# Reordering the first stage of an attention and MLP-mixer kernel

## The chip, the cores and the metric

The kernel runs on one NeuronCore of a Trainium2 chip, launched once. The metric is device time in microseconds of one execution. Five engines run side by side, each with its own instruction list: TensorE (PE) multiplies matrices, VectorE (DVE) and ScalarE (ACT) work on tiles in SBUF and PSUM, GpSimd (POOL) works on tiles in SBUF, and SyncE (SP) issues most of the DMA transfers. ACT and POOL issue transfers too. PE writes its results to PSUM, which has eight banks of 128 x 512 fp32.

## The reference

There are 8 batches, 8 heads, 576 positions and 64 elements per head. The first half is a linear attention with a norm, the second an MLP mixer:

```python
kv = np.einsum('bhsd,bhse->bhde', k, v)
out = np.einsum('bhsd,bhde->bhse', q, kv)
rms = np.sqrt(np.mean(out * out, axis=-1, keepdims=True) + 1e-06)
x = out / rms * g_norm                      # then (B, S, H*D) = 8 x 576 x 512
xt = x.transpose(0, 2, 1)
h = np.maximum(xt @ w_tok1, 0.0) @ w_tok2   # 576 -> 256 -> 576
u = x + h.transpose(0, 2, 1)
h2 = np.maximum(u @ w_ch1, 0.0) @ w_ch2     # 512 -> 1536 -> 512
return u + h2
```

The activations are fp32. The weights come in as 8-byte words and are turned to fp32 in the kernel.

## The kernel before

The batches are taken in pairs, four pairs in all. For a pair the kernel loads k, v and q, multiplies k and v to one 64 x 64 matrix per head (`kv`), evicts it (`evict`), multiplies q by it (`attend_tile`), squares and reduces the result to a root mean square, scales it to x, and then mixes tokens with w_tok1 and w_tok2. The last and longest part, the channel mixing with w_ch1 and w_ch2, follows for all batches. The change touches only the stage of the first pair, and what is loaded ahead of it.

A batch's k or v has 576 rows of 2 KB. The first 512 go to SBUF in one transfer, four rows to each of 128 partitions (8 KB pieces). The last 64 are the remainder, two transfers of 32 rows. `load(b)` issues them all: for batch 0 k on SP's queue and v on ACT's, for the others all on SP's. `load_q` fetches q's 512 positions (1 MB in 2 KB pieces), `load_q_rest` the other 64 (in 256 B pieces). Two batches have buffers at a time, so the loads of pair 1 wait for the products of pair 0.

A weight block is fetched as 8-byte words and decoded by five operations: two passes on ACT (`scale`), then `clamp`, `shift` and `add` on DVE. Before, w_tok1 has three blocks: rows 0 to 255, rows 256 to 511, and the remainder.

The order of the work in this stage is written out by hand. `start` is a list of step names that `play` takes one after the other. Each step puts its instructions at the end of its engines' lists, and each engine takes its list in order; an instruction waits by semaphores for what it reads. DMA transfers take eight semaphores in turn, so a transfer cannot be issued before the eighth one ahead of it has landed. The step names that matter, with side s (batch in the pair), tile c of x (two tiles of 128 positions for each c; c = 0, 1 are batch 0, c = 2, 3 batch 1, c = 4 the remainders) and half t:

- `kv`s h and `e`s h: the k and v products of one half of the heads, and their eviction.
- `a`c t: the product with q for one tile, into a PSUM bank of the pool "o", which has two.
- `g`c t: DVE multiplies the bank by g_norm into x (L453). `q`c t: ACT squares the bank (L457). `t`c t: DVE sums the squares (L474).
- `m`, `r`, `i`: mean on DVE (L479), square root on ACT (L484), inverse with one correction step on DVE (L488 to L493).
- `s`, `p` or `d` c t: x times the inverse, on ACT (eight instructions, L507), GpSimd (L515) or DVE (L511).
- `h`s t j: one product of w_tok1's block j with tile j of x, into a bank of the pool "h", which has four.
- `w`n k: step k of decoding block n (0 and 1 are w_tok1's two blocks, 2 its remainder, 3 and 4 w_tok2). `w`n 0 fetches.
- `l`, `lq`, `lr`: loads for the next pair. `gs` spreads g_norm over the partitions by a product with ones. `j`n: n products with an identity matrix whose result nobody reads.

Every PE product of fp32 operands is two records in the profile.

## Time and profile before

| what | us |
|---|---|
| three runs | 772.5, 770.87, 772.44 |
| median | 772.44 |
| profiled execution, its own time | 771.12 |
| its span, first to last instruction | 769.3 |
| PE busy in the span | 759.4 |
| DVE busy | 642.5 |
| ACT busy | 277.4 |
| GpSimd busy | 112.3 |

The first stage is the first 46 us or so. A line of the timeline gives the start, the time until the end of the last of the merged instructions, the engine, the line of the kernel, the operation, what it writes and reads, the count, and in brackets the idle time before it with what ended it. A line of the stretches gives the stretch, its length, busy time and instructions of PE, PE's weight loads, DVE, ACT and POOL, then the granted clock of PE, the busy share of the DMA engines and the rate in GB/s. Ends of matmuls are modelled, so a short wait of PE can be hidden in a row that looks busy; the spacing of starts shows it.

### The profile page before, as it was taken

Reading aid. Unit: us, or ns where it says so; the run is one execution under the profiler, and the core shown is the slowest. Engines: PE = TensorE matmul, PEld = TensorE weight load, DVE = VectorE, ACT = ScalarE, POOL = GpSimd, SP = SyncE. Lnnn points to the kernel's source line nnn. Section 1 sums busy time; section 2 is a strip of 40 time slices with the busy share of each in tenths; the row PEclk is TensorE's granted clock in tenths of the full one; section 3 lists DMA queues with packets and bytes.
Section 4 is the critical chain, followed back from the end, with each engine's and each line's share of the span. In section 5 each row is a group of like instructions: output and inputs, shape, how many; then the busy total and the mean of one; then the engine's idle time right before and its main releaser. Section 6 shows DMA issues by size and latency. Waiting matters only on the chain.

```text
span 769.3 us, 12678 instructions
## 1 busy us (share of the span) xinstructions
PE 759.4 (99%) x4676; PEld 612.3 (80%) x4676; DVE 642.5 (84%) x945; ACT 277.4 (36%) x556; POOL 112.3 (15%) x125
## 2 busy tenths in 40 slices
PE   7999999999999999999999999999999999999998
PEld 6665555445888888888888888888888888888887
DVE  3868897997767779899969889987998996798996
ACT  3555575764210233511244242123352223325221
POOL 1003020213410000002240001042000218000204
PEclk9999999999999999999999999999999999999999
DMA  9999998499699786589998577999659879955679
GB/s 339 366 366 370 373 372 301 151 318 342 251 286 339 271 282 191 164 270 207 216 236 251 158 224 216 255 188 267 202 148 290 172 220 208 207 145 157 151 200 119
DMA packets 137677, 188.26 MB, mean 245 GB/s; under 512 B 48658, under 2 KB 95250, under 8 KB 135570
## 3 DMA queue, kind: packets, MB, share of 16 engines
q1 hardware_dynamic: 101744, 167.54, 68.9%
q0 software_dynamic: 34816, 18.36, 16.1%
q10 hardware_dynamic: 1058, 1.57, 0.6%
q8 instruction: 37, 0.61, 0.3%
q14 instruction: 22, 0.18, 0.1%
HBM read 138.28 MB, written 49.15 MB: 244 GB/s over the span
## 4 chain that ended last, share of the span: by engine, by line
PE 97%; DMA 2%; SPq 0%; issue 0%; DVE 0%
PE ps_d L136 28%; PE ps_b L136 19%; PE ps_a L136 19%; PE ps_u L136 8%; PE ps_h L136 8%; PE ps_v L136 5%; PE ps_c L136 3%; DMA v_in<-in_v_dram 2%; PE ps_kv L136 2%; PE ps_o L136 2%; PE ps_w L136 2%; SPq L124 0%; PE ps_r L136 0%; DVE xs L127 0%
## 5 line engine op out<-in xcount | busy, mean ns | idle before, releaser
L136 PE MATMUL ps_d<-ui,w 128*128 128x256 f32 x504 | 118.6, 379 | 0.0
L136 PEld LDWEIGHTS ps_d<-ui,w 128*128 128x128 f32 x504 | 95.9, 190 | 12.9
L133 ACT COPY ps_d<-ps_a 128x768 f32<-128x768 f32 (+1 forms) x56 | 32.0, 572 | 200.2 <-PE ps_a L136 197.2
L127 DVE TENSOR_TENSOR v<-v,v 128x1536 f32<-128x1536 f32 (+2 forms) x70 | 103.2, 1482 | 0.3
L136 PE MATMUL ps_b<-sv,w 128*128 128x256 f32 x324 | 78.9, 380 | 0.0
L136 PE MATMUL ps_a<-v,w 128*128 128x256 f32 x324 | 78.8, 379 | 0.0
L1206 POOL DMA_DIRECT2D out_dram<-us x24 | 26.7, 1833 | 291.8 <-ACT p L133 286.2
L136 PEld LDWEIGHTS ps_b<-sv,w 128*128 128x128 f32 x324 | 61.3, 190 | 8.8 <-issue 0.6
L136 PEld LDWEIGHTS ps_a<-v,w 128*128 128x128 f32 x324 | 61.7, 190 | 8.2
L136 PE MATMUL ps_u<-h,w_tok 128*128 128x512 f32 (+1 forms) x160 | 64.7, 599 | 0.0
L136 PE MATMUL ps_d<-v,w 128*128 128x256 f32 x258 | 62.7, 379 | 0.0
L130 ACT ACTIVATE v<-v 128x768 f32<-128x768 f32 (+1 forms) x54 | 42.6, 822 | 55.1 <-DVE v L127 52.3
L136 PE MATMUL ps_h<-x,w_tok 128*128 128x512 f32 x128 | 57.8, 600 | 0.7 <-DVE w_tok L190 0.7
L1206 POOL DMA_DIRECT2D out_dram<-r x40 | 41.3, 1927 | 102.0 <-ACT p L133 80.3
L136 PE MATMUL ps_d<-sv,w 128*128 128x256 f32 x228 | 55.4, 379 | 0.0
L136 PEld LDWEIGHTS ps_d<-v,w 128*128 128x128 f32 x258 | 49.0, 190 | 6.5
L136 PEld LDWEIGHTS ps_u<-h,w_tok 128*128 128x128 f32 (+1 forms) x160 | 25.6, 179 | 31.1 <-issue 26.7
L136 PEld LDWEIGHTS ps_d<-sv,w 128*128 128x128 f32 x228 | 43.4, 190 | 5.8
L136 PE MATMUL ps_a<-uT,w 128*128 128x256 f32 x192 | 46.7, 379 | 0.0
L136 PEld LDWEIGHTS ps_h<-x,w_tok 128*128 128x128 f32 x128 | 23.4, 190 | 27.1 <-issue 24.1
L136 PE MATMUL ps_b<-ui,w 128*128 128x256 f32 x168 | 40.8, 379 | 0.0
L136 PEld LDWEIGHTS ps_a<-uT,w 128*128 128x128 f32 x192 | 36.5, 190 | 4.9
(169 smaller groups left out, 1288.0 us busy)
## 6 DMA issues: line engine op xcount, KB each, us to landing
w<-parts SPq DMA_DIRECT2D x168, 384.0 KB
w<-parts SPq DMA_DIRECT2D x56, 192.0 KB
uT<-blocks SPq DMA_DIRECT2D x36, 256.0 KB
k_in<-in_k_dram SPq DMA_DIRECT2D x8, 1024.0 KB
qT<-in_q_dram SPq DMA_DIRECT2D x8, 1024.0 KB
out_dram<-x POOLq DMA_DIRECT2D x16, 512.0 KB, 7.0
v_in<-in_v_dram SPq DMA_DIRECT2D x7, 1024.0 KB
raw<-in_moe_w_ch_dram SPq DMA_DIRECT2D x8, 768.0 KB
```

What stands on the lines that cost most here:

```text
L127: keep(engine.tensor_tensor(out=o, in0=a, in1=b, op=op))
L130: keep(nc.scalar.activation(o, a, AF.Relu))
L133: keep(nc.scalar.copy(o, a))
L136: keep(nc.tensor.matmul(*a, **kw))
L1206: keep(nc.gpsimd.dma_start(to, t()[ds(b * Q, Q), at].rearrange("p n l j -> p n (l j)"), accum_op=ALU.add))
```

## The change

- The loads of batch 0 all go on SP's queue, in this order: k's rows, v's rows, k's remainder, v's remainder. g_norm's row is fetched on POOL's queue instead of ACT's, ahead of everything else there.
- w_tok1's first block is split in two (rows 0 to 127 and 128 to 255). The first half is fetched after v's remainder and ahead of batch 0's q, the second after that q. The second block is fetched after batch 1's k and v instead of before them.
- `kv` is split by rows: `ka` multiplies the 512 rows, `kb` the remainder. Both halves of the heads do `ka` before `kb`.
- The second half of the first kv is evicted by ACT instead of DVE.
- For c = 0 and 1 the gain is taken apart: `y` copies the bank to x on ACT, `n` multiplies x by g_norm on GpSimd. DVE's `g` is gone there.
- The two tiles of c = 0 have statistics of their own (`m00`, `r00`, `i00` and `m01`, `r01`, `i01`) instead of common ones.
- `a10` and `a11` write to banks of the pool "h", so that the first four tiles have four banks.
- For c = 0 the second tile is scaled by GpSimd (`p01`) instead of ACT; for c = 1 the second tile by ACT (`s11`, placed after `q21`) instead of DVE. For c = 2 and 3 the square comes before the gain.
- The identity matrix is replaced by a full tile of ones, set by DVE. The unused products are 21, 5 and 4 instead of 12 and 8.

```diff
-    ident = inp.tile([P, P], F32, name="ident")
+    ones = inp.tile([P, P], F32, name="ones")
...
+    def load_rows(dst, t, b):
+        dma(dst[:, :J], t[b, :LO].rearrange("(p j) e -> p j e", j=J))
+
+    def load_rem(dst, t, b):
+        for n in range(0, HF, Q):
+            dma(dst[n:n + Q, J], t[b, LO + n:LO + n + Q].rearrange("(r e) d -> e r d", e=8))
...
-        queues = (nc.sync, nc.sync if b else nc.scalar)
-        for dst, t, e in zip((k_in[b % 2], v_in[b % 2]), (k, v), queues):
-            dma(dst[:, :J], t[b, :LO].rearrange("(p j) e -> p j e", j=J), e)
-            for n in range(0, HF, Q):
-                dma(dst[n:n + Q, J], t[b, LO + n:LO + n + Q].rearrange("(r e) d -> e r d", e=8), e)
+        pairs = ((k_in[b % 2], k), (v_in[b % 2], v))
+        if b:
+            for dst, t in pairs:
+                load_rows(dst, t, b)
+                load_rem(dst, t, b)
+        else:
+            for f in (load_rows, load_rem):
+                for dst, t in pairs:
+                    f(dst, t, b)
...
+    def get_tok1_half(j):
+        return block(DTOK, lambda raw: [(raw, words(moe_w_tok1)[ts(j, P)])], w_tok1[0][:, j])
...
-        def kv(side, half):
+        def kv(side, half, js=range(JJ)):
...
-                for j in range(JJ):
+                for j in js:
...
-            if whole and side == 0:
+            if whole and side == 0 and half == 0:
                 keep(nc.vector.tensor_copy(o, i))
             else:
                 copy(o, i)
...
-            o = ps["o"].tile([P, DM], F32, name="ps_o", tag="o")
+            n = "h" if c == 1 else "o"
+            o = ps[n].tile([P, DM], F32, name="ps_o", tag=n)
...
+        def take(c, h):
+            if (pair, c) not in X:
+                X[pair, c] = xps[pair % 2].tile([P, 2, DM], F32, name="x", tag="x2", bufs=4)
+            copy(X[pair, c][:, h].rearrange("p (h d) -> p h d", d=D), bank[c, h])
+
+        def gain_pool(c, h):
+            x = X[pair, c][:, h].rearrange("p (h d) -> p h d", d=D)
+            keep(nc.gpsimd.tensor_mul(x, x, g_sb.to_broadcast([P, H, D])))
...
+        alone = lambda c: whole and c == 0
...
+            if alone(c):
+                g = h
+                stat[g] = [stats.tile([P, H, 1], F32, name=name + str(h)) for name in ("ms", "root", "inv")]
+                keep(nc.vector.tensor_reduce(stat[g][0], sq[c, h], axis=AX.X, op=ALU.add))
+                return
...
+    first_rows = [get_tok1_half(j) for j in range(2)]
...
+    dma(g_row, bass.AP(tensor=g_norm.tensor, offset=g_norm.offset, ap=[[0, 1], list(g_norm.ap[0])]), nc.gpsimd)
     load(0)
+    first_rows[0][0]()
     load_q(0)
-    for block in tok1[:2]:
-        block[0]()
+    first_rows[1][0]()
     load(1)
+    tok1[1][0]()
     load_q(1)
...
     start = [
-        "j12 kv00 e00", "kv01 gs e01 l0", "a00 g00 q00", "a01 g01 q01 t00 t01 m0 w01",
-        "a10 w02 r0 i0 w03 d00 w04 q10 w30 w40 lq0", "a11 q11 s01 g10 g11 w11 j8",
-        "h000 h010 w12 w13 w14 t10 t11 m1 r1", "kv10 e10", "kv11 e11 i1 d10 d11 l1", "h001", "a20 q20", "h011",
-        "a21 q21 g20 g21 t20 t21 m2", "h002 h012 r2", "a30 g30 i2 d20 q30", "a31 q31 s21 g31 t30",
+        "j21 ka00 ka01 kb00 e00 kb01 e01 gs l0 w01 w02 w03 w04 j5",
+        "a00 q00 y00 n00 t00 m00 r00 i00 d00", "a01 q01 y01 n01 t01", "a10 q10 y10 n10 m01 r01 w51 i01 p01 w30 w40 lq0",
+        "a11 q11 y11 n11 w52 w53 w54 w11 t10 t11 m1 j4",
+        "h000 h010", "kv10 e10", "kv11 e11 r1 w12 w13 i1 d10 w14 l1", "h001", "a20 q20", "h011",
+        "a21 q21 s11 g20 g21 t20 t21 m2", "h002 h012 r2", "a30 q30 g30 i2 d20", "a31 q31 s21 g31 t30",
         "h003 h013 t31 m3",
         "a40 q40 r3 i3 d30 s31 g40 t40 m4 r4 w21 i4 d40 lr0 lr1"]
...
-            matmul(o[:, :P], lhsT=ident, rhs=ident, start=True, stop=True)
-
-    more |= {f"j{n}": do(keep_warm, n) for n in (8, 12)}
+            matmul(late["junk"][:, :P], lhsT=ones, rhs=ones, start=True, stop=True)
+
+    more |= {f"j{n}": do(keep_warm, n) for n in (4, 5, 21)}
```

In the new list block 0 is the first half of the old first block (`w0`), block 5 the second half (`w5`).

More of the change, by code (lines that the diff above doesn't have):

```diff
@@ L9 @@
 from concourse.dve_ops import ADD32_U16LIMBS
-from concourse.masks import make_identity
 F32 = mybir.dt.float32
@@ L97 @@
           for n, b in (("o", 2), ("kv", 2), ("h", 4))}
-    ident = inp.tile([P, P], F32, name="ident")
+    ones = inp.tile([P, P], F32, name="ones")
     g_sb = inp.tile([P, 1, D], F32, name="g_sb")
-    g_row, ones = (inp.tile([1, n], F32, name=name) for n, name in ((D, "g_row"), (P, "ones")))
+    g_row = inp.tile([1, D], F32, name="g_row")
     w_tok1 = [tokw.tile([P, 2, DTOK], F32, name=f"w_tok1{i}") for i in range(J // 2)]
@@ L164, in decode, with high, low, scale @@
         bits = dst.bitcast(U32)
-        def scale():
+        def high():
             keep(nc.scalar.activation(dst, raw()[..., 1].bitcast(F32), AF.Prelu,
                                       scale=2.0 ** -112, alpha=2.0 ** 32))
-            low = raw()[..., 0]
-            keep(nc.scalar.activation(low, low, AF.Copy, scale=2.0 ** -29))
+        def low():
+            t = raw()[..., 0]
+            keep(nc.scalar.activation(t, t, AF.Copy, scale=2.0 ** -29))
+        def scale():
+            high()
+            low()
         def scale_leaves():
@@ L190, in add @@
             keep(nc.vector._custom_dve(ADD32_U16LIMBS, out=o, in0=o, in1=flat().bitcast(U16)[..., 2 * leaves:][..., :2]))
-        return scale_leaves if leaves else scale, clamp, shift, add
+        return scale_leaves if leaves else scale, clamp, shift, add, high, low
     def words(w):
@@ L371, in attention @@
         whole = pair == 0
-        def kv(side, half):
+        def kv(side, half, js=range(JJ)):
             kk, vv = k_in[side], v_in[side]
-            if whole:
+            if js[0]:
+                o = kv_ps[side, half]
+            elif whole:
                 o = kv_ps[side, half] = zeroed[half]
@@ L378, in kv @@
                 o = kv_ps[side, half] = ps["kv"].tile([P, 2, P], F32, name="ps_kv", tag="kv")
+            split = len(js) < JJ
             for i in range(2):
-                for j in range(JJ):
+                for j in js:
                     for h in range(2):
@@ L384, in kv @@
                                rhs=vv[:, j, at],
-                               start=(j == 0), stop=(j == JJ - 1), skip_group_check=True)
+                               start=(j == 0 and not (split and i)), stop=(j == JJ - 1), skip_group_check=True)
         def evict(side, half):
@@ L495, in inv_of @@
         def inv_of(c, t):
+            if alone(c):
+                return stat[t][2].rearrange("p (k h) o -> p k h o", h=2)
             inv = stats_of(c)[2]
@@ L519, in attention @@
             for h in range(2):
-                steps |= {f"kv{s}{h}": do(kv, s, h), f"e{s}{h}": do(evict, s, h),
+                steps |= {f"ka{s}{h}": do(kv, s, h, range(J)), f"kb{s}{h}": do(kv, s, h, range(J, JJ)),
+                          f"kv{s}{h}": do(kv, s, h), f"e{s}{h}": do(evict, s, h),
                           f"l{s}": do(load, 2 * pair + 2 + s)}
@@ L532, in attention @@
                 steps |= {f"{n}{c}{t}": do(f, c, t) for n, f in zip("spd", (scale, scale_pool, scale_vector))}
+        if whole:
+            for h in range(2):
+                steps |= {f"m0{h}": do(mean, h), f"r0{h}": do(sqrt, h), f"i0{h}": do(invert, h)}
+                for c in range(2):
+                    steps |= {f"y{c}{h}": do(take, c, h), f"n{c}{h}": do(gain_pool, c, h)}
         for g in groups:
@@ L1250, in stream @@
         for n in range(len(blocks)):
-            clamp, shift, add = blocks[n][2:]
+            clamp, shift, add = blocks[n][2:5]
             if n + 1 < len(blocks):
@@ L1287 @@
     zeroed = [ps["kv"].tile([P, 2, P], F32, name="ps_kv", tag="kv") for _ in range(2)]
+    keep(nc.vector.memset(ones, 1.0))
     for t in zeroed:
@@ L1293 @@
     keep(nc.scalar.activation(root, root, AF.Sqrt))
-    make_identity(nc, ident)
-    keep(nc.gpsimd.memset(ones, 1.0))
-    dma(g_row, bass.AP(tensor=g_norm.tensor, offset=g_norm.offset, ap=[[0, 1], list(g_norm.ap[0])]), nc.scalar)
     def spread_g():
         o = ps["h"].tile([P, DM], F32, name="ps_g", tag="h")
-        matmul(o[:, :D], lhsT=ones, rhs=g_row, start=True, stop=True)
+        matmul(o[:, :D], lhsT=ones[:1], rhs=g_row, start=True, stop=True)
         copy(g_sb[:, 0], o[:, :D])
     start = [
[4 rows of a table removed]
[5 rows of a table added]
         "h003 h013 t31 m3",
@@ L1333 @@
     mixings.append(token_mixing(B // 2 - 1, range(2, 9), (0, 1)))
-    more = {f"w{n}{k}": f for n, b in enumerate(tok1 + tok2) for k, f in enumerate(b)}
+    more = {f"w{n}{k}": f for n, b in enumerate(first_rows[:1] + tok1[1:] + tok2 + first_rows[1:]) for k, f in enumerate(b)}
     more |= {f"f{n}": b[0] for n, b in enumerate(channel)}
@@ L1341, in keep_warm @@
     def keep_warm(n):
-        o = ps["h"].tile([P, DM], F32, name="ps_j", tag="h")
+        if n > 4:
+            late["junk"] = ps["h"].tile([P, DM], F32, name="ps_j", tag="h")
         for _ in range(n):
-            matmul(o[:, :P], lhsT=ident, rhs=ident, start=True, stop=True)
-    more |= {f"j{n}": do(keep_warm, n) for n in (8, 12)}
+            matmul(late["junk"][:, :P], lhsT=ones, rhs=ones, start=True, stop=True)
+    more |= {f"j{n}": do(keep_warm, n) for n in (4, 5, 21)}
     more["gs"] = spread_g
```

## The prediction

> **What bounds the kernel now.** I read the page first: TensorE (PE) is busy in 759.4 of 769.3 us, and the chain that ended last is 97% PE.

> ```profile
> span 769.3 us, 12678 instructions
> PE 759.4 (99%) x4676; PEld 612.3 (80%) x4676; DVE 642.5 (84%) x945; ACT 277.4 (36%) x556; POOL 112.3 (15%) x125
> PE   7999999999999999999999999999999999999998
> PE 97%; DMA 2%; SPq 0%; issue 0%; DVE 0%
> ```

> Only the first slice of PE is below 9, so whatever the first stage can give lies in the first 25 us. The change edits nothing behind that stage. If PE reaches some instruction x us earlier and never waits after it, the kernel ends x us earlier. The question is which instruction that is. PE's rows in the timeline, with the idle time in brackets:

> ```profile
> 8.81 0.69 PE L136 MATMUL ps_kv<-v_in,k_in 128*64 128x64 f32 x16 [0.85 <-DMA v_in<-in_v_dram]
> 12.19 2.05 PE L136 MATMUL ps_o<-kvp,qT 128*128 128x128 f32 x16
> 16.72 1.95 PE L136 MATMUL ps_j<-ident 128*128 128x128 f32 x16
> 19.35 1.99 PE L136 MATMUL ps_h<-x,w_tok 128*128 128x512 f32 x4 [0.68 <-DVE w_tok L190]
> 21.67 2.55 PE L136 MATMUL ps_kv<-v_in,k_in 128*64 128x64 f32 x80 [0.34 <-DMA v_in<-in_v_dram]
> 24.16 1.13 PE L136 MATMUL ps_h<-x,w_tok 128*128 128x512 f32 x2
> 25.24 1.13 PE L136 MATMUL ps_o<-kvp,qT 128*128 128x128 f32 x8
> 26.20 1.02 PE L136 MATMUL ps_h<-x,w_tok 128*128 128x512 f32 x2
> 27.07 1.05 PE L136 MATMUL ps_o<-kvp,qT 128*128 128x128 f32 x8
> ```

> The reader is to see the pair at 24.16 and 25.24: one product of two records, then `a20`, 1.08 us later. The same pair at 26.20 and 27.07 is 0.87 us apart. So `a20` waited about 0.2 us, which the model of matmul ends hides. `a20` is the first reader of q1 (batch 1's q). In the trace the semaphore of q1 has its last increment at 25.11, `a20`'s weight load starts at 25.21. Behind it PE's rows are spaced as their counts demand.

> Then the loads, by stretches (the last columns are granted clock, DMA share, GB/s):

> ```profile
> 3.00:7.00 4.00, 3.66 (x17) 3.66 (x18) 0.00 (x0) 1.49 (x2) 0.43 (x2) 1.00 1.02 408
> 10.50:13.50 3.00, 3.00 (x62) 2.87 (x58) 0.89 (x3) 0.21 (x1) 0.00 (x0) 1.00 0.99 305
> 13.50:19.50 6.00, 4.73 (x40) 4.35 (x39) 5.66 (x14) 5.03 (x14) 0.00 (x0) 1.00 1.03 412
> 19.50:22.50 3.00, 2.66 (x32) 1.38 (x34) 2.85 (x6) 1.52 (x4) 0.00 (x0) 1.00 1.03 380
> 22.50:25.20 2.70, 2.70 (x61) 1.88 (x57) 2.25 (x8) 0.85 (x3) 0.00 (x0) 1.00 1.22 268
> ```

> The DMA engines are full from 3 us on until q1 has landed. That is the second bound: what lands when is a matter of the bytes put ahead of it.

> **The change part by part.**

> Issue. ACT's three v0 issues go to SP, and a fourth load is put ahead of q0. SP took 2.07 us for its first three, so q0 is issued at about 0.75 + 6 x 0.69 + 0.45 = 5.3 us, not 2.87. Nothing is lost by it: the k0 and v0 rows, 2.1 MB at 408 GB/s from 2.5 us, hold the engines until 7.7. ACT's saved 2.4 us are worth nothing; ACT waits 7.6 us there until 12.30. [...]

> First kv. Before, 2.25 MB of k0 and v0 shared the engines with q0's start and PE began at 8.81, then waited 0.32 for remainders. Rows first: 8.3 to 8.8; I take 8.5, as the 42 junk records also end about there (DVE sets `ones` at 0.9 us, so from 1.1: 27 at the half-rate spacing of 0.213 until 6.88, when the trace shows the full clock, and 15 at 0.111, makes 8.5). The 80 records need 2.55 us, so kv ends at 11.1 instead of 11.83.

> q0. It has 0.26 MB of w_tok1 ahead of it that it had not: 0.64 us at 408 GB/s, 0.86 at the 305 of the stretch where w_tok1 was read. It landed at 12.02 and will at 12.7 to 12.9. `a00` starts at 12.9 instead of 12.19: 0.7 us later, and the five junk products wait in front of it for nothing.

> First x. From `a00` 12.9: product 1.0, square 0.60 (14.5), copy to x 0.6 on ACT (15.1); reduce 0.68 and mean 0.17 on DVE beside it (15.4), root 0.21, the four small operations of `i0` 0.85 (16.5). GpSimd's gain from 15.1 takes 1.25 (row of `p`, 1246 ns; 1.03 to 1.55 seen): 16.4. `d00` 0.69: 17.2. `h000`, which waited for the w_tok decode until 19.35, now starts at 17.2 to 17.9: 1.5 to 2.1 us earlier. The four PSUM banks end the 0.59 us wait for `sq` before `a10`. The extra statistics (five small DVE operations, 1.0 us) lie on a DVE that gives four gains (2.8 us) to GpSimd.

> Second kv. k1 and v1 have 0.52 MB less ahead of them: at 380 GB/s they land 1.4 us earlier, and kv10 starts at 20.3 instead of 21.67. `h000`, `h010` end by 19.7, so PE idles about 0.6 us. kv10, kv11 end at 22.9, `h001` (needs GpSimd's `p01`: `n10` and `p01` at 1.25 behind `i01` give 21) at 23.8.

> `a20`. Up to here PE is 1.4 us ahead. But q1 has ahead of it exactly the bytes of before: k0, v0, k1, v1 4.72 MB, q0 1.05, the 512 rows of w_tok1 1.05, and its own 1.05; only their order differs. The stretch was full before, so q1 lands at 25.1 again and `a20` starts at 25.2. PE's 1.4 us are spent as idle time in front of it. There is a second limit just below: ACT's `w11` now stands in front of `e10`, `e11` and waits for the second half of w_tok1, which lands right before q1: 21.9 to 22.4, plus 1.33 for the two decode passes, plus two copies of 0.36 gives 24.1 to 24.6.

> Behind `a20`. PE's list is the same to the end. On ACT `s11` (2.02) moves between `q21` and `q30`. From the rows: `q21` ends 28.82, `s11` 30.9, `r2` 31.2 (it waits for `m2` at 30.93 anyway), `q30` 31.8, `g30` on DVE 32.5, `i2` 0.98, `d20` 0.69: 34.2. Before, `d20` ended at 33.11; `h100` reads it at 34.30. Bounds 0 to 0.3 us; I take 0.05. `w14` ends by 27.2, `h002` wants it at 27.96.

> Junk: ten more products, all in waits of PE: 0.

> Sum: a20 from 25.24 to 25.2, plus 0.05: no change. Span 769.3, the profiled execution 771.1 again; that execution is 1.3 us below the median of 772.44, so I say 772.3 for a median.

> **Rivals.**

> B, q1 a little earlier. Its 16 increments come at 22.0 to 22.9 (seven) and 23.7 to 25.11 (nine), with 24.64 and 25.11 behind the rest. If the stragglers vanish, ACT's limit decides: -0.6 to -1.1 us, 771.4. For it: the last two look accidental. Against: nothing in the change takes bytes off the late engines.

> C, the whole advance passes. If q1 landed by 23.6, kv10's 1.4 us, or `h000`'s up to 2.1, would reach the end: 770.7. For it: 305 GB/s at 10.5 to 13.5 shows 0.3 MB, 0.75 us, lost while w_tok1 is read, and another order may lose less. Against: ACT's limit at 24.1 must fall too.

> D, slower: PE's clock. PE idles some 0.6 us before kv10 and up to 1.4 us before `a20`. At the start PE ran at half rate from 3.34 to 6.88. If the idle time brings that back once for as long, 3.5 us of work at half rate cost 1.75 us: 774.1. It decides from the point where the granted clock drops; the 0.85 us at 7.96 did not drop it, and the longest gap here is 1.4 us. [...]

> E, slower: ACT's queue. If w_tok1's second half lands after 23.1 (at the 268 GB/s of the last stretch), `w11` holds `e10`, `e11` past 25.2: landing at 24 puts `a20` at 26.1, +0.9, and up to +1.6 at 24.7: 773.5. Against: 19.5 to 22.5 ran at 380.

> That the loads don't change order can't be: SP's list is in program order.

> **How the numbers follow.** A, q1 decides: 0.58. B 0.17, C 0.12, D 0.06, E 0.07. A measurement of this kernel tells about 0.2% (1.5 us) from no change; the three runs of before spread over 1.6 us. Faster: C, a quarter of B, and 0.03 of A by scatter: 0.19. Slower: D, two thirds of E, and 0.03 of A: 0.14. The range goes from C's 770.7 to D's 774.0. A's own is 771.8 to 773.0.

> **What would show it.** After: kv's first row at 8.3 to 8.8; `a00` at 12.5 to 13.2; `h000` at 17 to 18; kv10 near 20.3; an idle stretch of PE of about 1.4 us that ends with `a20` at 25.0 to 25.5, released by qT; GpSimd rows of about 1.25 us; `h100` 9.1 us after `a20`; granted clock 1.00 throughout. `a20` before 24 means that q1 was not bound by bytes, and I am wrong towards faster. `a20` after 26, or a clock below 1.00 between 19 and 30, means slower.

## The result, and the profile after

| what | before | after |
|---|---|---|
| median, us | 771.33 (9 runs) | 773.62 (9 runs) |
| profiled execution, its own time | 771.12 | 772.95 |
| its span | 769.30 | 770.88 |

The changed kernel is slower: the ratio is 1.0026, with an interval of 1.0016 to 1.0036 that excludes 1; the medians are 2.3 us apart. Nine runs put the kernel before at 771.33; the median of 772.44 shown above came from three, two of them high. The profiled execution of the changed kernel is the fastest of its nine, so its 1.83 us over the profiled execution of before is a lower figure. The span gives 1.58 of them, what lies around the span 0.25.

The page of the changed kernel:

```profile
span 770.9 us, 12741 instructions
...
PE 762.0 (99%) x4696; PEld 614.2 (80%) x4696; DVE 643.9 (84%) x948; ACT 280.4 (36%) x564; POOL 118.9 (15%) x128
...
PE   8999999999999999999999999999999999999997
...
PE 96%; DVE 2%; DMA 1%; SPq 1%; issue 0%; ACT 0%; DVEq 0%
```

As before, only the first and the last slice of PE are below 9. But DVE now holds 2% of the chain that ended last, and SP's queue 1%; before both had 0%. PE's rows in the timeline of the changed kernel:

```profile
8.21 2.55 PE L135 MATMUL ps_kv<-v_in,k_in 128*64 128x64 f32 x80
...
13.09 3.81 PE L135 MATMUL ps_o<-kvp,qT 128*128 128x128 f32 x32 [0.65 <-DMA qT<-in_q_dram]
...
18.74 1.98 PE L135 MATMUL ps_h<-x,w_tok 128*128 128x512 f32 x4 [0.95 <-DVE x L552]
20.66 2.55 PE L135 MATMUL ps_kv<-v_in,k_in 128*64 128x64 f32 x80
24.41 1.10 PE L135 MATMUL ps_h<-x,w_tok 128*128 128x512 f32 x2 [1.20 <-DVE w_tok L206]
25.34 1.05 PE L135 MATMUL ps_o<-kvp,qT 128*128 128x128 f32 x8
...
28.77 1.98 PE L135 MATMUL ps_h<-x,w_tok 128*128 128x512 f32 x4 [0.63 <-DVE w_tok L206]
...
34.19 1.09 PE L135 MATMUL ps_r<-kvp,qR 128*64 128x128 f32 x16
```

PE's two waits in the first kv (0.85 us ahead of it, 0.32 for a remainder) are gone, and kv10 comes at 20.66 instead of 21.67, straight behind `h010`. `h001` (24.41) and `h002` (28.77) now wait for DVE's last step of a w_tok1 block, L206. `a20` (25.34) starts 0.43 us behind the second record of `h001`, the spacing of rows without a wait; in the trace q1's last increment is at 24.88 already. So it is L206, by way of `h001`, that sets `a20` here, and not q1. The last row, the first product of the remainders (`ps_r`), is the mark that I use for the end of the stage: from its start to PE's last matmul it is 732.28 us in the kernel before (33.27 to 765.55) and in the changed one (34.19 to 766.47). So the stage lost 0.92 us, and the other 0.66 us of the span lie behind PE's last matmul: 3.75 us before, 4.41 after.

The stretches of the changed kernel, with the columns as before:

```profile
3.00:7.00 4.00, 4.00 (x26) 4.00 (x25) 0.00 (x0) 0.00 (x0) 0.92 (x2) 1.00 1.01 426
10.50:13.50 3.00, 2.35 (x26) 2.05 (x22) 1.44 (x4) 1.23 (x4) 0.00 (x0) 1.00 1.07 418
13.50:19.50 6.00, 5.05 (x41) 4.58 (x40) 4.07 (x9) 3.22 (x7) 2.71 (x2) 1.00 1.00 403
19.50:22.50 3.00, 3.00 (x65) 2.04 (x65) 2.59 (x7) 2.62 (x7) 2.39 (x3) 1.00 1.08 360
22.50:25.20 2.70, 1.50 (x28) 1.05 (x23) 2.58 (x4) 0.99 (x3) 1.48 (x2) 1.00 1.14 264
```

The DMA engines are full all the way, the granted clock is full, and PE's idle time of 1.2 us before `h001` is the 1.50 busy of 2.70 in the last line. In the same line DVE is busy for 2.58 us with four instructions. Its rows in the timeline, and GpSimd's:

```profile
15.61 1.17 DVE L518 TENSOR_SCALAR ms<-ms 128x8 f32<-128x8 f32 x1
...
20.36 0.72 DVE L528 SCALAR_TENSOR_TENSOR ms<-ms,inv 128x8 f32<-128x8 f32 x1
...
21.71 1.15 DVE L201 TENSOR_SCALAR w_tok<-w_tok 128x256 uint32<-128x256 uint32 x1
22.97 1.29 DVE L206 CUSTOM_DVE_ANT_1 w_tok<-w_tok,raw 128x512 uint16<-128x512 uint16 x1
24.18 1.26 DVE L513 TENSOR_REDUCE ms<-sq 128x8 f32<-128x512 f32 x2
...
28.03 0.69 DVE L206 CUSTOM_DVE_ANT_1 w_tok<-w_tok,raw 128x1024 uint16<-128x1024 uint16 x1
```

```profile
15.48 1.27 POOL L485 TENSOR_TENSOR x<-x,g_sb 128x512 f32<-128x512 f32 x1 [11.56 <-ACT x L132]
18.05 2.99 POOL L485 TENSOR_TENSOR x<-x,g_sb 128x512 f32<-128x512 f32 x2 [1.31 <-ACT x L132]
21.66 1.05 POOL L556 TENSOR_TENSOR x<-x,inv 128x512 f32<-128x512 f32 x1 [0.61 <-DVE inv L532]
22.66 1.32 POOL L485 TENSOR_TENSOR x<-x,g_sb 128x512 f32<-128x512 f32 x1
```

A mean over 128x8 numbers (L518) takes 1.17 us, and it ends at 16.78, when GpSimd's multiplication ends (16.75). L528 ends at 21.08 with GpSimd's pair (21.04), L201 at 22.86, L206 at 24.26, each within 0.3 us of the end of a GpSimd row. Where GpSimd does nothing the same four take 0.17, 0.17, 0.29 and 0.43 (rows further down, of the runs without multiplications on GpSimd). With a second L518 of 0.52 that is 3.6 us in which DVE was held. What had begun ahead of the multiplication was not held: L552 at 18.00 took its 0.69 us, and there the multiplication, which began 0.05 us later, took 1.76 us instead of 1.27. DVE has no idle stretch over 0.3 us from 14.9 until 28.7: it has become the bound of the stage.

### The profile page after: what moved, and what is told of

Same layout as the page of the kernel before. It is cut to its first block, busy times and chain, and to the rows that moved or that the text cites. A ratio compares the mean times of both kernels' runs of the same rounds, so it can differ in the third digit from the quotient of the medians.

```text
span 770.9 us, 12741 instructions
## 1 busy us (share of the span) xinstructions
PE 762.0 (99%) x4696; PEld 614.2 (80%) x4696; DVE 643.9 (84%) x948; ACT 280.4 (36%) x564; POOL 118.9 (15%) x128
## 4 chain that ended last, share of the span: by engine, by line
PE 96%; DVE 2%; DMA 1%; SPq 1%; issue 0%; ACT 0%; DVEq 0%
PE ps_d L135 28%; PE ps_b L135 19%; PE ps_a L135 19%; PE ps_u L135 8%; PE ps_h L135 8%; PE ps_v L135 5%; PE ps_c L135 3%; PE ps_o L135 2%; PE ps_w L135 2%; PE ps_kv L135 2%; DMA qT<-in_q_dram 1%; SPq L123 1%; PE ps_r L135 0%; DVE w_tok L206 0%; DVE ms L518 0%; DVE w_tok L201 0%
## 5 line engine op out<-in xcount | busy, mean ns | idle before, releaser
L135 PEld LDWEIGHTS ps_h<-x,w_tok 128*128 128x128 f32 x128 | 23.3, 190 | 29.5 <-issue 23.8
```

What stands on the lines that cost most here:

```text
L135: keep(nc.tensor.matmul(*a, **kw))
```

## The experiments

Two theories of the stage. P: DVE is held by GpSimd's multiplications, and that makes the two waits for L206. L: DVE's list is too long or in a worse order by itself (ten small operations in place of five, decodes behind them). On the end behind PE's last matmul, T: PE's longer list brings one more fetch of instructions among the last stores; G: g_norm's row on another queue.

**The changed kernel once more, without an edit**

> The changed kernel once more, unchanged, to see what of its profile repeats. Theory P (DVE operations are held while GpSimd multiplies): DVE rows that overlap a GpSimd multiplication are stretched again (mean 1.2 us instead of 0.17, decode steps 1.1 to 1.3 us instead of 0.29 and 0.43), the product h001 waits about 1.2 us and h002 about 0.6 us for the w_tok decode, and the last PE row ends 0.9 us later than before. Theory L (DVE's list is merely longer and in a worse order): the two waits repeat, the stretched rows need not. Both: about 1.0025 of the kernel before. The tail behind the last PE row, 3.75 us before and 4.41 after in one profile each: if it is 4.4 again it belongs to the change, if it is near 3.8 it is scatter.

773.30 us, ratio 1.0024 (1.0015 to 1.0033); `h001` waits 1.19, `h002` 0.62, `ps_r` at 34.54, 4.02 us behind PE's last matmul. The waits repeat to 0.01 us; `ps_r` moves by 0.35, as the first q landed later (`a00` at 13.45 instead of 13.09). q1's last increment is at 24.90 and `a20` at 25.69, again 0.43 us behind the second record of `h001`.

**No multiplication on GpSimd**

```diff
-        "a00 q00 y00 n00 t00 m00 r00 i00 d00", "a01 q01 y01 n01 t01", "a10 q10 y10 n10 m01 r01 w51 i01 p01 w30 w40 lq0",
-        "a11 q11 y11 n11 w52 w53 w54 w11 t10 t11 m1 j4",
+        "a00 q00 g00 t00 m00 r00 i00 d00", "a01 q01 g01 t01", "a10 q10 g10 m01 r01 w51 i01 d01 w30 w40 lq0",
+        "a11 q11 g11 w52 w53 w54 w11 t10 t11 m1 j4",
```

> The changed kernel with the gain of the first four tiles back on DVE (one multiplication from the bank instead of copy on ACT and multiplication on GpSimd) and tile c=0, t=1 scaled by DVE: GpSimd does nothing in the stage, DVE does 3.4 us more. Theory P: no DVE row is stretched, 3.6 us of holding vanish, h001 does not wait for the decode, a20 starts at q1's landing (25.0 to 25.4), h002 at most 0.3 us late, and the kernel is 0.6 to 1.0 us faster than the changed one, about level with the kernel before. Theory L: DVE has 3.4 us more to do, h001 and h002 are later still, 1 to 3 us slower than the changed kernel.

772.65 us, ratio 1.0017 (1.0008 to 1.0026). From DVE's and PE's rows:

```profile
23.09 0.29 DVE L201 TENSOR_SCALAR w_tok<-w_tok 128x256 uint32<-128x256 uint32 x1
23.42 0.43 DVE L206 CUSTOM_DVE_ANT_1 w_tok<-w_tok,raw 128x512 uint16<-128x512 uint16 x1
```

```profile
23.90 1.13 PE L135 MATMUL ps_h<-x,w_tok 128*128 128x512 f32 x2 [0.77 <-DVE w_tok L206]
25.18 1.13 PE L135 MATMUL ps_o<-kvp,qT 128*128 128x128 f32 x8
...
28.28 1.98 PE L135 MATMUL ps_h<-x,w_tok 128*128 128x512 f32 x4 [0.22 <-DVE w_tok L206]
```

DVE has five operations more, 3.4 us of work, and yet ends its L206 earlier than in the changed kernel: no row is stretched. `h002` waits 0.22 instead of 0.63, and `ps_r` comes at 33.70. P had `h001` without a wait; it waits 0.77 us, but q1 covers that (last increment 25.04, `a20` 25.18). The work that GpSimd took off DVE cost DVE more than it saved.

**Three GpSimd multiplications more, read by nobody**

```diff
+    def extra():
+        keep(nc.gpsimd.tensor_mul(idle, idle, g_sb.to_broadcast([P, 6, D])))
...
-        "a00 q00 y00 n00 t00 m00 r00 i00 d00", "a01 q01 y01 n01 t01", "a10 q10 y10 n10 m01 r01 w51 i01 p01 w30 w40 lq0",
-        "a11 q11 y11 n11 w52 w53 w54 w11 t10 t11 m1 j4",
+        "a00 q00 y00 n00 px t00 m00 r00 i00 d00", "a01 q01 y01 n01 t01", "a10 q10 y10 n10 m01 r01 w51 i01 p01 w30 w40 lq0",
+        "a11 q11 y11 n11 px px w52 w53 w54 w11 t10 t11 m1 j4",
...
+    more["px"] = extra
```

> The changed kernel with three more GpSimd multiplications (128 x 384, about 0.95 us each) on a scratch tile that nobody reads: one behind the first gain, two behind the fourth. No instruction waits for them but GpSimd's own next ones, which have idle time ahead of them. Theory P: the correction step of the first inverse is held until the first extra one ends (d00 up to 0.8 us later), and mean, clamp and shift between 25 and 27 us are held by the other two: h002 waits 1 to 2 us more, the kernel 1 to 2 us slower than the changed one. Theory L: no change within 0.3 us.

774.43 us, ratio 1.0035 (1.0021 to 1.0049); `ps_r` at 35.61. DVE's list is unchanged, but `d00`, 0.69 us in the changed kernel, is held too, and `h000` comes at 20.14. `h002` waits 1.19 us, 0.56 more than in the changed kernel, where P had 1 to 2 more:

```profile
18.50 1.59 DVE L552 TENSOR_TENSOR x<-x,inv 128x512 f32<-128x512 f32 x1
```

**Common statistics for the first two tiles, as before**

```diff
-        alone = lambda c: whole and c == 0
+        alone = lambda c: False
...
-        "a00 q00 y00 n00 t00 m00 r00 i00 d00", "a01 q01 y01 n01 t01", "a10 q10 y10 n10 m01 r01 w51 i01 p01 w30 w40 lq0",
+        "a00 q00 y00 n00 t00", "a01 q01 y01 n01 t01 m0 r0 i0 d00", "a10 q10 y10 n10 w51 p01 w30 w40 lq0",
```

> The changed kernel with common statistics for the two first tiles, as before (five small DVE operations and one ACT root less). GpSimd's multiplications stay. Theory L: DVE's list is 1 us shorter and free of one round trip over ACT, h001 and h002 wait at least 1 us less, and the kernel comes to the level of the one before. Theory P: h000 is 1 to 2 us later, as it needs both tiles' sums; the GpSimd multiplications still hold two to four DVE operations for 1.5 to 3 us in all, and h002 is still late by 0.3 us or more.

773.19 us, ratio 1.0023 (1.0014 to 1.0032). Here `h000` comes at 20.18 and kv10 at 22.09, 1.4 us later than in the changed kernel. And yet `h001` and `h002` wait for nothing, and `ps_r` is at 33.50, earlier than there. DVE was still held (L197 1.13, L201 1.25 and L552 1.29 us), but its list had five small operations less and its decodes stood further ahead. (Its time is still above that of before: 4.65 us lie behind PE's last matmul.) So holding alone does not make the loss; it needs a list without room for it.

**The gains left out.** GpSimd's five multiplications are left out, so the first tiles of x lack the gain and `x01` its scale. All other lists are those of the changed kernel.

```diff
-        "a00 q00 y00 n00 t00 m00 r00 i00 d00", "a01 q01 y01 n01 t01", "a10 q10 y10 n10 m01 r01 w51 i01 p01 w30 w40 lq0",
-        "a11 q11 y11 n11 w52 w53 w54 w11 t10 t11 m1 j4",
+        "a00 q00 y00 t00 m00 r00 i00 d00", "a01 q01 y01 t01", "a10 q10 y10 m01 r01 w51 i01 w30 w40 lq0",
+        "a11 q11 y11 w52 w53 w54 w11 t10 t11 m1 j4",
```

> The changed kernel with GpSimd's five multiplications left out (the four gains and the scaling p01, so the first tiles of x are not multiplied); DVE's list, ACT's and PE's are those of the changed kernel. It prices the holding alone. Theory P: no DVE row between 14 and 24 us is longer than the same row alone (L518 0.17, L528 0.17, L201 0.29, L206 0.43 or 0.7 for the wide one), DVE's list is some 3 us shorter, h001 and h002 wait for no decode of w_tok, a20 at 25.0 to 25.4 (q1's bytes), ps_r at 33.2 to 33.6. Rival L (DVE's list is too long for the stage by itself): h001 or h002 still waits 0.4 us or more for w_tok and ps_r is at 33.9 or later.

772.32 us, ratio 1.0011 (1.0002 to 1.0019).

```profile
22.60 1.12 PE L135 MATMUL ps_h<-x,w_tok 128*128 128x512 f32 x2
25.38 1.13 PE L135 MATMUL ps_o<-kvp,qT 128*128 128x128 f32 x8 [1.65 <-DMA qT<-in_q_dram]
...
28.10 1.88 PE L135 MATMUL ps_h<-x,w_tok 128*128 128x512 f32 x4
...
33.41 1.09 PE L135 MATMUL ps_r<-kvp,qR 128*64 128x128 f32 x16
```

```profile
16.08 0.17 DVE L518 TENSOR_SCALAR ms<-ms 128x8 f32<-128x8 f32 x1
...
16.76 0.17 DVE L528 SCALAR_TENSOR_TENSOR ms<-ms,inv 128x8 f32<-128x8 f32 x1
...
20.20 0.29 DVE L201 TENSOR_SCALAR w_tok<-w_tok 128x256 uint32<-128x256 uint32 x1
20.61 0.42 DVE L206 CUSTOM_DVE_ANT_1 w_tok<-w_tok,raw 128x512 uint16<-128x512 uint16 x1
```

This is the prediction's own picture: `h001` directly behind kv11, then 1.65 us of idle time until q1 has landed, `a20` at 25.38, no wait for DVE. The stage ends 0.14 us behind that of before; what is left of the loss lies at the end, 4.77 us behind PE's last matmul. P holds and L alone falls: the list has room where it is not held. L206 ends at 21.03 here and at 24.26 in the changed kernel, 3.2 us apart, while kv11 ends at 22.6: there were 1.6 us to spare.

**Twenty unused products, as before the change**

```diff
-        "j21 ka00 ka01 kb00 e00 kb01 e01 gs l0 w01 w02 w03 w04 j5",
+        "j16 ka00 ka01 kb00 e00 kb01 e01 gs l0 w01 w02 w03 w04",
...
```

> The changed kernel with twenty junk products (sixteen and four) in place of thirty, as many as the kernel before has. Theory T (the end is later because PE's list is longer: a 38th packet of 16384 bytes on queue 8 lands at 764 us, among the last stores): that packet is gone, 37 are left with the last near 748, and the stretch from PE's last matmul to the end of the span is 3.7 to 3.9 us instead of 4.0 to 5.1; PE's last matmul at 766.4 to 766.9 as in the changed kernel, or later where the clock rises later for the missing junk; the time 0.3 to 1.2 us below the changed kernel's. Theory G (the end is later for another reason, such as g_row's fetch that left ACT's queue): the stretch stays at 4.0 to 5.1 us, whatever the packets do.

773.45 us, ratio 1.0027 (1.0016 to 1.0037): as slow as the changed kernel. The stretch behind PE's last matmul is 4.13 us. That is in G's range and not in T's, although the packet that T named is gone. The page's rows of the two instruction queues, before, after, and here:

```profile
q8 instruction: 37, 0.61, 0.3%
q14 instruction: 22, 0.18, 0.1%
```

```profile
q8 instruction: 38, 0.62, 0.3%
...
q14 instruction: 23, 0.19, 0.1%
```

```profile
q8 instruction: 37, 0.61, 0.3%
...
q14 instruction: 23, 0.19, 0.1%
```

That packet (16384 bytes on queue 8, 0.9 us of one DMA engine, at 764 us in the changed kernel) is no longer there, and the stores land as in the kernel before. The rest lies on SP, whose list is 855 entries long, not 850 (v0's three loads, one more for the split block, one wait). In all fifteen profiles the trace has a step of 0.36 to 0.38 us in front of SP's 848th entry. In the kernel before that is between the closing drains, where a step takes 0.16 us here. In the lists of 855 it falls among the closing waits, which are otherwise 0.06 to 0.09 us apart, and the drains follow with steps of their own. The last step is 0.46 us here and 0.23 in the kernel before; what it waits for is not shown. The 23rd packet on queue 14 (8192 bytes) is not one more: the page counts what starts inside the span, and the last packet starts at 770.60 here, 0.40 us ahead of the end, and at 769.55 in the kernel before, 0.25 us behind it. So T is half right: a second term, the length of SP's list, is added.

**g_norm's row back on ACT's queue**

```diff
-    dma(g_row, bass.AP(tensor=g_norm.tensor, offset=g_norm.offset, ap=[[0, 1], list(g_norm.ap[0])]), nc.gpsimd)
+    dma(g_row, bass.AP(tensor=g_norm.tensor, offset=g_norm.offset, ap=[[0, 1], list(g_norm.ap[0])]), nc.scalar)
```

> The changed kernel with g_row's fetch back on ACT's queue. Theory G: the stretch from PE's last matmul to the end of the span is back at 3.7 to 3.9 us, and the time 0.3 to 1.2 us below the changed kernel's. Theory T: the packet at 764 us is still there, the stretch is 4.0 to 5.1 us and the time level with the changed kernel's within 0.5 us.

773.46 us, ratio 1.0027 (1.0017 to 1.0036); the packet at 764 us is there and the stretch is 4.46 us. G falls.

**The kernel before with one part of the change: w_tok1's second block behind batch 1's k and v**

```diff
-    for block in tok1[:2]:
-        block[0]()
+    tok1[0][0]()
     load(1)
+    tok1[1][0]()
...
-        "a11 q11 s01 g10 g11 w11 j8", "h000 h010 w12 w13 w14 t10 t11 m1 r1", "kv10 e10", "kv11 e11 i1 d10 d11 l1",
+        "a11 q11 s01 g10 g11 j8", "h000 h010 t10 t11 m1 r1 i1 d10 d11", "kv10 e10", "kv11 e11 w11 w12 w13 w14 l1",
```

> The kernel before with one thing of the change: the second block of w_tok1 (half a megabyte) is fetched behind batch 1's k and v, and w11 to w14 moved behind e11; statistics, gains, banks and junk as before. Theory Q (the bytes ahead of batch 1's q decide when a20 starts): k1 and v1 land about 1.3 us earlier, kv10 starts at 20.9 to 21.3 as soon as h000 and h010 are done, PE then waits about 1 us, a20 at 25.0 to 25.5 as before; the time is level with the kernel before, within 0.3 us. Theory R (the order of loads gains by itself and only the work on DVE and GpSimd lost it): a20 before 24.6, the time 0.6 to 1.3 us below the kernel before.

771.26 us, ratio 1.0001 (0.9990 to 1.0013), level.

```profile
21.27 2.55 PE L136 MATMUL ps_kv<-v_in,k_in 128*64 128x64 f32 x80
23.75 1.12 PE L136 MATMUL ps_h<-x,w_tok 128*128 128x512 f32 x2
25.15 1.13 PE L136 MATMUL ps_o<-kvp,qT 128*128 128x128 f32 x8 [0.28 <-DMA qT<-in_q_dram]
```

kv10 is 0.4 us earlier, and `a20` gets nothing of it: now the view itself names q1 as what it waits for. Theory Q, the prediction's case A, holds by itself.

**The same, with batch 1's q in halves**

g_norm's row is also fetched on POOL's queue here.

```diff
-            dma(qT[b], q[b].rearrange("(c p) s -> p c s", p=P)[..., :LO])
+            parts = [slice(0, LO)] if b != 1 else [slice(0, LO // 2), slice(LO // 2, LO)]
+            for part in parts:
+                dma(qT[b][..., part], q[b].rearrange("(c p) s -> p c s", p=P)[..., part])
```

> The run before this one with batch 1's q loaded in two halves by columns, so that a20 and a21 need the first half alone, and g_row fetched by GpSimd. Theory Q: half of the 1.05 MB is no longer ahead of a20, 1.3 us at 408 GB/s and up to 1.9 us at the 268 GB/s of that stretch; PE has 0.5 to 1.0 us to take up, since kv11 and h001 end about 24.2, so a20 starts at 24.2 to 24.7, and the time is 0.4 to 1.0 us below the kernel before. Theory R: q's bytes are not the limit, a20 starts where it does in the run with the late block alone, and the times are level within 0.3 us.

771.59 us, ratio 1.0000 (0.9992 to 1.0009). `a20` starts at 24.94 and no longer waits: PE is busy from `h000` (19.58) on, and DVE's work in front of `h000` is the next bound. `ps_r` is at 32.89, 0.38 us earlier than before, but the stretch behind PE's last matmul is 4.18 us: SP's list has one entry more (851). Another 0.48 us were lost on the way, in front of one product of the second pair's remainders, where PE waits for nothing that the profile shows:

```profile
61.21 0.27 PE L136 MATMUL ps_r<-kvp,qR 64*64 64x64 f32 x1 [0.21 <-issue]
```

So the gain was given back twice, at 61 us and at the end. The first loss is in no other profile, and its cause is open.

**The first block decoded in two parts, SP's list as long as before**

```diff
-                dma(dst[n:n + Q, J], t[b, LO + n:LO + n + Q].rearrange("(r e) d -> e r d", e=8), e)
+                dma(dst[n:n + Q, J], t[b, LO + n:LO + n + Q].rearrange("(r e) d -> e r d", e=8),
+                    e if b or not n else nc.scalar)
...
+            t = lambda: raw[0][:, ts(j, DTOK)]
+            return decode(w_tok1[0][:, j], t, t)
...
-        "a10 w02 r0 i0 w03 d00 w04 q10 w30 w40 lq0", "a11 q11 s01 g10 g11 j8",
+        "a10 w02 r0 i0 w03 d00 w04 w51 q10 w52 w53 w54 w30 w40 lq0", "a11 q11 s01 g10 g11 j5",
```

The late block, the halves of q and g_norm's row on POOL are as in the run before this one.

> The kernel before with batch 1's q in halves and the late block (as in the run with halves), and two edits more: the first block of w_tok1 is decoded in two parts of 256 columns, the part that h000 reads first, with five junk products in place of eight in front of it; and k0's second remainder is issued by ACT, so that SP's list has again as many instructions as in the kernel before. Theory D (DVE's work in front of h000 sets the whole stage once q1's bytes don't): 0.7 us less of it, h000 at 18.7 to 19.0 instead of 19.58, kv10 at 20.6 to 21.0, a20 at 24.0 to 24.5, the stage behind it 0.5 to 0.8 us earlier than in the run with halves. Rival: q's first half or v1's remainders land too late, a20 stays at 24.9. Theory S (the 0.33 us pause in SP's closing row of waits is a matter of how long SP's list is): the stretch from PE's last matmul to the end of the span is 3.7 to 3.8 us, not the 4.18 of the run with halves. Both together: 0.8 to 1.3 us below the kernel before.

772.37 us, ratio 1.0022 (1.0008 to 1.0035), slower. S holds: 850 entries, 3.78 us. D could not show: ACT issued k0's remainder ahead of v0's rows, kv's first row came at 10.40 behind 2.06 us of idle time, and then the granted clock fell to half from 11.10 to 14.51.

**The same with v0's rows first on ACT**

```diff
-        for dst, t, e in zip((k_in[b % 2], v_in[b % 2]), (k, v), queues):
+        pairs = list(zip((k_in[b % 2], v_in[b % 2]), (k, v), queues))
+        for dst, t, e in pairs if b else pairs[::-1]:
```

> The run with the first block decoded in two parts again, with ACT's issues in another order: v0's rows and remainders first and k0's second remainder last, since the first try put k0's remainder ahead of v0's rows and PE's first kv came at 10.40 us. Theory D: kv's first row at 8.6 to 8.9, no drop of the clock, h000 at 18.9 to 19.3 instead of 19.58, kv10 at 20.8 to 21.2, a20 at 24.2 to 24.6, ps_r (the stage's end) at 32.2 to 32.6 against 33.27; the stretch behind PE's last matmul 3.7 to 3.8 us; time 0.6 to 1.1 us below the kernel before. Rival: batch 1's q or v lands too late for it, a20 at 24.9 and the time level within 0.4 us.

770.90 us, ratio 1.0000 (0.9991 to 1.0009); 3.79 us behind PE's last matmul, `ps_r` at 32.83. k0's remainder was late again (PE waits 1.03 us for it at 10.43), so `h000` came at 19.51 and `a20` at 24.87, not at 24.2 to 24.6. From `a00` to `h000` it is 6.71 us instead of 7.15, which is D's mechanism at 0.44 us, not 0.7. The span is 0.4 us shorter than that of before, and the times are level: no version here beats the kernel before by what can be measured.

**What is left of the change without GpSimd, without own statistics, with twenty unused products**

```diff
-        alone = lambda c: whole and c == 0
+        alone = lambda c: False
...
-        "j21 ka00 ka01 kb00 e00 kb01 e01 gs l0 w01 w02 w03 w04 j5",
-        "a00 q00 y00 n00 t00 m00 r00 i00 d00", "a01 q01 y01 n01 t01", "a10 q10 y10 n10 m01 r01 w51 i01 p01 w30 w40 lq0",
-        "a11 q11 y11 n11 w52 w53 w54 w11 t10 t11 m1 j4",
+        "j16 ka00 ka01 kb00 e00 kb01 e01 gs l0 w01 w02 w03 w04",
+        "a00 q00 g00 t00", "a01 q01 g01 t01 m0 r0 i0 d00", "a10 q10 g10 w51 d01 w30 w40 lq0",
+        "a11 q11 g11 w52 w53 w54 w11 t10 t11 m1 j4",
...
```

> The changed kernel without GpSimd's multiplications, without the first tiles' own statistics and with twenty junk products: what is left of the change is the order of the loads on SP, the first kv in two parts, the fourth bank and the moved s11. Theory P (the loss in the stage is DVE's: held by GpSimd, and five small operations more): ps_r, the stage's end, at 33.1 to 33.5 as in the kernel before (33.27); no row of DVE stretched. Rival L (the loads or ACT's order cost too): ps_r at 33.8 or later. The stretch behind PE's last matmul stays at 4.1 us in both (SP's longer list). Time 0.3 to 0.7 us above the kernel before by P, 0.9 or more by L.

772.93 us, ratio 1.0017 (1.0007 to 1.0026); `ps_r` at 34.73, later than P has it. The stretches of this run:

```profile
10.06:13.47 3.41, 1.05 (x26) 0.85 (x21) 1.44 (x4) 1.23 (x4) 0.00 (x0) 1.00 1.06 392
13.47:16.89 3.42, 3.33 (x15) 3.36 (x16) 0.61 (x2) 0.60 (x1) 0.00 (x0) 0.50 1.01 417
```

PE had no unused products in front of `a00` and idled for 2.45 us there; then the granted clock was 0.50 for 3.42 us, and the first 32 records of attention took 5.40 us instead of 3.81.

**The same with thirty unused products**

```diff
-        "j16 ka00 ka01 kb00 e00 kb01 e01 gs l0 w01 w02 w03 w04",
+        "j21 ka00 ka01 kb00 e00 kb01 e01 gs l0 w01 w02 w03 w04 j5",
```

> The run with the loads alone, with the changed kernel's thirty junk products back (five of them in front of a00). Theory W (that run's half clock from 13.47 to 16.89 us came of PE's 2.45 us of idle time in front of a00, and cost 1.6 us): the clock stays full from 7 us on, the 32 records of the first products of attention take 3.8 us, not 5.40. Theory P: ps_r at 33.2 to 33.6, as with the gains left out. Rival L: ps_r at 33.9 or later with the clock full. The 38th packet at 764 us comes back and the stretch behind PE's last matmul is 4.0 to 5.1 us. Time 0.4 to 1.2 us above the kernel before by P, 1.4 or more by L.

772.98 us, ratio 1.0021 (1.0010 to 1.0032). W holds: no drop at 13 us, 3.81 us for the 32 records. But `h000` now waits 1.88 us for the common statistics, and the clock falls there:

```profile
17.35:20.76 3.41, 1.53 (x8) 0.89 (x8) 2.96 (x10) 1.82 (x5) 0.00 (x0) 1.00 1.02 390
20.76:24.17 3.41, 3.41 (x35) 1.91 (x35) 3.27 (x10) 1.23 (x2) 0.00 (x0) 0.50 1.11 295
```

`h000`, `h010` and kv10 take 2.78 and 3.31 us where they take 1.98 and 2.55. Less these 1.56 us `ps_r` would be at 33.07. In the run before this one, 34.73 less 1.59 is 33.14, but its q1 landed at 25.43; with `a20` 0.13 us behind that and `ps_r` 7.96 us behind `a20`, as in its rows, it could not come before 33.5. Both are near the 33.27 of the kernel before. These are estimates from the rows; no run showed the loads alone at full clock throughout.

## Why the prediction was wrong

The time of 773.62 is inside the range, but the likeliest case was no change, and the kernel is slower. That the range holds it is luck: its upper end was worked out from D, the clock, which did not occur.

**Right.** The first kv (8.5 forecast, 8.21 measured, just under its 8.3 to 8.8), `a00` (12.9, 13.09), q1's last increment (25.1, 24.88), the clock (full). Case A, that the bytes ahead of q1 set `a20` and the advance dies there, stands in the run with the late block and, purest, in the run with the gains left out, which ends its stage 0.14 us from that of before.

**Right by luck.** kv10 (20.3, 20.66) comes straight behind a late `h010`, without the 0.6 us of idle time that was forecast. `a20` (25.2, 25.34) was to end an idle stretch of 1.4 us, released by qT. The idle stretch of 1.2 us lies in front of `h001`, and L206 ends it; q1 had landed 0.46 us before `a20` (0.13 in the kernel before).

**Wrong, the stage: 0.92 us.** The step that failed is the one that costed "First x" and "`w14` ends by 27.2, `h002` wants it at 27.96". It put GpSimd's gains at 1.25 us each beside DVE rows at their lone durations, and called DVE relieved ("gives four gains (2.8 us) to GpSimd"). The rows show a DVE that is held for 3.6 us. `h000` came at 18.74 instead of 17.2 to 17.9; 1.0 us of that is L518's 1.17. `h001` came at 24.41, where the forecast has it start at 22.9, with the end of kv11, and end at 23.8; and it came behind L206 instead of `p01`. The slack in front of q1 took up most of this, and 0.10 us reached `a20`. `w14` ended at 28.72, 1.5 us after the forecast, and `h002` waited 0.63 us: from `a20` to `h002` it is 3.43 us against 2.72 before. That 0.71, 0.10 at `a20` and 0.11 behind `h002` are the 0.92. The trace of before has a hint: at 107.8 us a multiplication on GpSimd (L515) stands beside a DVE L181 of 1.42 us on 128x768; the mean of the eight of that shape is 0.65, which leaves 0.54 for the other seven.

**Wrong, the end: 0.66 us.** "Nothing is lost by it" (the issues) and "ten more products, all in waits of PE: 0" were costed where they stand, at the start. Their price came 760 us later. "Only the first slice of PE is below 9" overlooks the last one, which is at 8 in the page of before. By the profiles with 850 entries on SP (3.75, 3.76, 3.78, 3.79 us behind the last matmul) and those with 851 or 855 and 37 packets on queue 8 (4.13, 4.18, 4.12), SP's longer list costs 0.37 us. With 38 on queue 8 it is 4.02 to 5.11 in eight profiles, 4.53 in the mean: between -0.1 and 1.0 us more, 0.4 in the mean. That SP's list is the cause of the first is shown by the two runs that add to the one with 851 entries and have 850 again. That PE's longer list is the cause of the second is not shown: the packet goes with the number of products, but the time saved by taking ten away was not measurable (773.45 against 773.46 and 773.30), since that run's stage was no earlier.

**Two sums.** ACT's limit in front of `a20` (21.9 to 22.4, plus 1.33, plus two copies of 0.36) comes to 23.95 to 24.45, not to 24.1 to 24.6. The 772.3 stands on the median of three runs, which nine runs put 1.1 us lower. Neither decided.

**Rivals.** D, the clock, was priced at 1.75 us and did not occur in the changed kernel. It occurred in three of the experiments, and cost 1.59 and 1.56 us in the two where the rows show it. B, C and E did not come: q1 landed where A has it, and ACT's `w11` was done at 22.86.

**DVE beside GpSimd.** L518 and L201 (one input and the output in SBUF, 1.17 and 1.15 us), L528, L552 and L206 (two inputs in SBUF, 0.72, up to 1.59 and 1.29 us) were held; L508 and L513 (reductions, 0.67 to 0.69) were not, nor was L527 (a reciprocal, 0.20 at 20.12 in the changed kernel, beside GpSimd's pair), nor L552 where it began first (0.69). In the changed kernel L518, L528, L201 and L206 took 1.00, 0.55, 0.86 and 0.86 us more than where GpSimd does nothing, and the GpSimd instruction beside them still had 1.14, 0.68, 1.00 and 1.01 us to run when they began. So the price was close to the rest of that instruction. Why these forms were held and the others not is not shown.

## What to carry to other kernels

Work given to GpSimd was not free for DVE here (3.6 us of holding): before moving a multiplication there, list the DVE operations that will start while it runs, and cost each, reductions and reciprocals apart, at the rest of the GpSimd instruction. An advance in front of a transfer that decides is only slack, and a change that adds work elsewhere can spend more than the slack. Instructions cost at the end of the list too: here one to five entries more on SP cost 0.37 us in the last microseconds, 760 us after the place where they were added.

## What the runs showed of the hardware that I had not expected

**Half clock lasted 3.41 us at a time, and the stretch ahead of it was not idle.** Half clock began at a boundary of such stretches counted from the clock's rise (6.65, 10.06, 13.47 in the run with the loads alone) and lasted 3.41 to 3.42 us in all three runs. PE was busy for 1.05, 1.35 and 1.53 us of the stretch ahead, by modelled ends. In the run with the gains left out it was busy for 1.76 us, and in the one with twenty products for 2.01, and the clock stayed:

```profile
22.01:25.42 3.41, 1.76 (x27) 0.89 (x21) 2.81 (x10) 1.67 (x5) 0.00 (x0) 1.00 1.13 276
```

```profile
9.16:12.57 3.41, 2.01 (x59) 1.80 (x54) 1.06 (x4) 1.23 (x4) 0.00 (x0) 1.00 1.03 360
```

**The length of an instruction list shows at the end.** In all fifteen profiles the stretch behind PE's last matmul is 3.75 to 3.79 us with 850 entries on SP, 4.12 to 4.18 with more and 37 packets on queue 8, and 4.02 to 5.11 with more and 38.
